# Two MoE layers on the two row halves of TensorE instead of on its column halves

## The chip, the cores and the metric

The kernel runs on one core of a Trainium2 chip. Its time is the device time of one execution in microseconds (us). A profiled execution is taken apart from the timed ones; its span runs from the first to the last instruction. TensorE is called PE in the profile (PEld is its weight loads), VectorE DVE, ScalarE ACT, GpSimd POOL and SyncE SP.

## The reference

Attention with a threshold (8 batches, 8 heads, 576 tokens, head dimension 64), followed by a two-layer perceptron over all 4608 tokens:

```python
scores = scale * np.matmul(q, k.transpose(0, 1, 3, 2))
thresh = np.max(scores, axis=-1, keepdims=True) - tau
scores = np.where(scores >= thresh, scores, -1e9)
attn = np.exp(scores - max); attn = attn / (sum + 1e-9)
x = np.matmul(attn, v)            # to (4608, 512)
h = x @ w_in                      # 512 -> 2048
out = np.maximum(0.01 * h, h) @ w_out   # 2048 -> 512
```

## The kernel before

The work is cut into 144 steps, 18 for each batch. A step takes two heads (a pair) and 128 queries: 16 steps cover the first 512 tokens, 2 "tail" steps the last 64 tokens of all eight heads. The loop at the end of the kernel (L487 to L534) runs over the steps n and issues, in this order, the work of several stages. Each engine's instructions stand in that order.

In step n, PE makes the scores of step n (`scores`, L217): q and k stand as high and low fp16 halves, so there are three products for each of two key halves and two heads, twelve matmuls. The heads of a pair lie in rows 0 to 63 and 64 to 127 of the array and run as a pair of matmuls, each on half of the rows and all 128 columns (64x128). DVE copies the scores out and takes the minimum of their negatives (`copy_min`, L225); POOL (DVE in the first 28 steps) makes the threshold (L232). ACT does two exponentials and a ramp for the step before (`exps`, L250 to L254), DVE the weights of one head (L263). Every second step the weights of two steps are turned by a DMA transpose (`turn_w`, L280) that SP issues, and four steps after the second of them, at the end of that step, PE multiplies them with v (`pv`, L303; PV_LAG = 4). DVE writes the result, with the normalizing factor, to the input x of the layers (`evacuate`, L325 and L315).

The layers work on groups of 256 tokens (128 for the tails of two batches). `layer1` (L346) makes one of eight units of h, 16 matmuls of 256 columns, followed by ACT's leaky ramp (L348); `layer2` (L362), twice a step, makes one eighth of the output of 128 tokens, four matmuls of 512 columns; ACT copies the output (L368) and SP stores it. Layer 2 of a group comes up once all units of layer 1 are issued. In both layers and in PV the output's 128 rows are split in two (`u2`), so that two matmuls run on the two column halves of the array (128 rows x 64 columns):

```python
nc.tensor.matmul(out=hp[ds(64 * u2, 64), jj, :], lhsT=w_in16[:, i, ds(128 * j + 64 * u2, 64)],
                 rhs=g.x[:, i, :], start=(i == 0), stop=(i == 3), skip_group_check=True)
```

q and k of the next batch are loaded by SP, split by POOL into high and low halves (`split_scale`, `split_high`, `split_low`), and turned by PE (`turn`, L177): 16 transposes per pair and operand (8 for the tails) into a PSUM tile `tp`, also on column halves, which DVE copies out (L188, L180). `turns_at`, `pool_at` and `loads_at` are dictionaries, written by hand, that say in which step each of these is issued.

PSUM tiles: `sc` two buffers, `h` two (hp, tp), `o` one, `pv` one.

Of the kernel before, what the change touches and what calls it, by code (L numbers as in the profile page):

```python
# [11 lines left out]
AX = mybir.AluOpType  # L12
AF = mybir.ActivationFunctionType

PV_LAG = 4


class Group:
# [20 lines left out]
def kernel(  # L39
# [122 lines left out]
    def turn(key, copy=None):  # L162
# [24 lines left out]
        else:  # L187
            copy(out=dst[:, :, p, ds(c0, 512)], in_=tp[:, :, :, :].rearrange("d x t p -> d x (t p)"))  # L188

    steps = []
# [9 lines left out]
    def scores(st):  # L202
        st.sc = [ps.tile([128, 2, 512], FP32, tag="sc", bufs=2, name=f"sc{h}") for h in range(2)]
        for kh in range(2):
            for i, (qx, kx) in enumerate(((0, 0), (1, 0), (0, 1))):
                for u in range(2 if st.tail else 1):
                    for h in range(2):
                        pair = st.p + u
                        rows = ds(64 * h, 64)
                        key0 = 64 * (1 - h) + 288 * kh  # L210
                        if st.tail:
                            lhs = turned[st.b, "q"][rows, qx, pair, MAIN:S]
                            o = st.sc[h][ds(64 * u, 64), kh, 0:288]
                        else:
                            lhs = turned[st.b, "q"][rows, qx, pair, ds(256 * st.blk + 128 * st.c, 128)]
                            o = st.sc[h][:, kh, 0:288]
                        nc.tensor.matmul(out=o, lhsT=lhs, rhs=turned[st.b, "k"][rows, kx, pair, ds(key0, 288)],  # L217
                                         start=(i == 0), stop=(i == 2), skip_group_check=True)

    def copy_min(st):  # L220

# [11 lines left out]

    def exps(st):

        c = 0 if st.tail else st.c
        if c == 0:
            pairs["now"] = pr = Pair()
            pr.w = sb.tile([128, 2, 10, 128], FP16, tag="w", bufs=3, name="w")
            pr.sum = sb.tile([128, 2, 2], FP32, tag="sum", bufs=3, name="sum")  # L240
            pr.n = 1 if st.tail else 2
        st.pair = pr = pairs["now"]
        flat = pr.w[:, c, :, :].rearrange("q n d -> q (n d)")
        st.w = [flat[:, ds(576 * h, 576)] for h in range(2)]
        st.sum = [pr.sum[:, c, h : h + 1] for h in range(2)]
        st.e = sb.tile([128, 576], FP16, tag="e", bufs=2, name="e")
        for h in range(2):
            if h:
                z = st.s[:, h, :]
                nc.scalar.activation(out=z, in_=z, func=AF.Prelu, bias=st.th[:, h, 0:1], scale=-1.0, alpha=1e20)  # L250
                nc.scalar.activation(out=st.w[h], in_=z, func=AF.Exp, bias=minus_tau[:, :], scale=1.0,  # L251
                                     accum_out=st.sum[h])
            else:
                nc.scalar.activation(out=st.e[:, :], in_=st.s[:, h, :], func=AF.Exp, bias=st.mn[:, h, 0:1],  # L254
                                     scale=-1.0)
# [38 lines left out]
    def pv(st):  # L294
        st.pv = ps.tile([128, 4, 128], FP32, tag="pv", bufs=1, name="pv")
        wt = st.pair.wt
        for u in range(2 if st.tail else 1):
            for i in range(5):
                for h in range(2):
                    blk = i if h == 0 else 9 - i  # L300
                    rhs = wt[:, 0, blk - (blk > 4), ds(64 * u, 64)] if st.tail else wt[:, :, blk - (blk > 4), :]
                    o = st.pv[ds(64 * h, 64), 0, ds(64 * u, 64)] if st.tail else st.pv[ds(64 * h, 64), 0:2, :]
                    nc.tensor.matmul(out=o, lhsT=v16[st.b % 2][:, st.p + u, blk, :], rhs=rhs,  # L303
                                     start=(i == 0), stop=(i == 4), skip_group_check=True)

    groups = {}
# [1 line left out]
    def evacuate(st, n):  # L308
        wt = st.pair.wt
        if st.tail:  # L310
            if (st.b % 2, st.c) == (0, 0):
                groups["t"] = xg = Group(128, (st.b, None))
                xg.x = sb.tile([128, NP, 128], FP16, tag="xt", bufs=2, name="xt")
            xg = groups["t"]
            nc.vector.tensor_tensor(  # L315
                out=xg.x[:, ds(st.p, 2), ds(64 * (st.b % 2), 64)],
                in0=st.pv[:, 0, :].rearrange("d (u q) -> d u q", u=2),
                in1=wt[:, 0, 9, :].rearrange("d (u q) -> d u q", u=2), op=AX.mult)
            done = (st.b % 2, st.c) == (1, 1)
# [13 lines left out]

    l1q, l2q, stores = [], [], []

    def layer1():
        g, u, nu, _ = l1q.pop(0)
        T, nj = g.tokens, 16 // nu
        if u == 0:
            g.g = sb.tile([128, 16, T], FP16, tag=f"g{T}", bufs=2 if T == 256 else 1, name="g")  # L340
        hp = ps.tile([128, nj, T], FP32, tag="h", bufs=2, name="hp")
        for jj in range(nj):
            j = nj * u + jj
            for i in range(4):
                for u2 in range(2):
                    nc.tensor.matmul(out=hp[ds(64 * u2, 64), jj, :], lhsT=w_in16[:, i, ds(128 * j + 64 * u2, 64)],  # L346
                                     rhs=g.x[:, i, :], start=(i == 0), stop=(i == 3), skip_group_check=True)
        nc.scalar.activation(out=g.g[:, ds(nj * u, nj), :], in_=hp[:, :, :], func=AF.Prelu,  # L348
                             bias=0.0, scale=1.0, alpha=0.01)
        if u == nu - 1:  # L350
            l2q.extend((g, m, r) for m in range(T // 128) for r in range(8))

    def layer2(n):
        g, m, r = l2q.pop(0)
        if r == 0 and n > N:

            g.o = ps.tile([128, 2, 512], FP32, tag="sc", bufs=2, name="osc")[:, 0, :]
        elif r == 0:
            g.o = ps.tile([128, 512], FP32, tag="o", bufs=1, name="o")
        for j in (2 * r, 2 * r + 1):  # L360
            for u2 in range(2):
                nc.tensor.matmul(out=g.o[ds(64 * u2, 64), :], lhsT=g.g[:, j, ds(128 * m + 64 * u2, 64)],  # L362
                                 rhs=w_out16[:, j, :], start=(j == 0), stop=(j == 15), skip_group_check=True)
        if r == 7:
            nm = g.tokens // 128
            if m == 0:
                g.osb = sb.tile([128, nm, 512], FP32, tag=f"osb{nm}", bufs=2 if nm == 2 else 1, name="osb")
            nc.scalar.activation(out=g.osb[:, m, :], in_=g.o[:, :], func=AF.Copy, bias=0.0, scale=1.0)  # L368
            if m == nm - 1:
                stores.append(g)  # L370

    def store():
        g = stores.pop(0)
# [12 lines left out]
    def at(d, n, f):  # L386
        d.setdefault(n, []).append(f)

    def units(b):
        u = [(b, p, w_) for p in range(NP) for w_ in "kq"]  # L390
        return u[:2] + [(b, "t", "k")] + u[2:] + [(b, "t", "q")]

    for b in range(1, B):
        base = PERB * (b - 1)
        for i, (s, w_) in enumerate(((0, "k"), (0, "q"), (1, "k"), (1, "q"))):
            at(loads_at, base + ((-2, 0, 5, 7)[i] if b > 1 else (3, 4, 8, 9)[i]),
               lambda b=b, s=s, w_=w_: load_main(b, s, w_))
        for i, w_ in enumerate("kq"):
            at(loads_at, base + (2, 12)[i] + 4 * (b == 1), lambda b=b, w_=w_: load_tails(b, w_))
        for i, key in enumerate(units(b)):  # L400
            n_ = base + 4 + 18 * i // 10 if b > 1 else 9 + 3 * i // 2
# [3 lines left out]
            at(turns_at, n_, lambda key=key: turn(key, nc.vector.tensor_copy))  # L405
    for b in range(B):
        base = PERB * (b - 1)
        if b:
# [73 lines left out]
        at(turns_at, n_, lambda key=key: turn(key, nc.vector.tensor_copy if key[2] == "q" else None))  # L482

    N = len(steps)
    pv_at = {s.n + PV_LAG - s.early: s for s in steps if s.tail or s.c == 1}
    n = 0
    while n < N + PV_LAG + 2 or l1q or l2q or stores:  # L487
        for f in loads_at.get(n, []):
# [21 lines left out]
        if 1 <= n <= N:  # L510
            last = steps[n - 1]
            weights(last)
            if last.early:
                recip(last.pair, last.c, 1)
                widen(last.pair, last.c, 1, nc.vector)
            elif last.tail or last.c == 1:
# [5 lines left out]
        if l1q and l1q[0][3] <= n:  # L522
            layer1()
        for f in turns_at.get(n, []):
            f()
        if 2 <= n < N + 2 and steps[n - 2].early:
            turn_w_pe(steps[n - 2].pair, steps[n - 2].c)
        for _ in range(2):
            if l2q:
                layer2(n)  # L530
        if n in pv_at:
            pv(pv_at[n])
            evacuate(pv_at[n], n)
        n += 1  # L534
# [1 line left out]
_INS = ['q', 'k', 'v', 'tau', 'moe_w_in', 'moe_w_out']  # L536
# [31 lines left out]
```

## Time and profile before

| | us |
|---|---|
| median of 3 runs | 515.27 (514.92 to 516.35) |
| the profiled execution | 515.1 |
| its span | 513.2 |
| PE busy | 488.5 |
| ACT busy | 433.4 |
| DVE busy | 423.8 |
| POOL busy | 305.3 |

The mean granted clock of PE was 0.992 of full speed. A busy PE is not PE at its peak: recorded matmuls overlap, and their ends are modelled. What a stage costs is read from the distance between starts.

### The profile page before, as it was taken

The numbers are of one execution on the slowest core, as the hardware profiler recorded it, in microseconds if no ns is written. First come the engines' busy times: TensorE is split into PE (matmuls) and PEld (weight loads), VectorE is DVE, ScalarE is ACT, GpSimd is POOL, SyncE is SP. The second block draws the span as 40 slices with busy tenths as digits, with TensorE's granted clock in tenths as the row PEclk, the third lists the DMA queues.
The fourth block names the chain that finished last, engine by engine and source line by source line (L and its number), as shares of the span: only waits on it lengthen the run. The fifth ranks groups of instructions, "written<-read, shape, count | busy, mean of one in ns | idle before, by whom it ended". The sixth has DMA issues, their size and how long they took to land.

```text
span 513.2 us, 19695 instructions
## 1 busy us (share of the span) xinstructions
PE 488.5 (95%) x8043; PEld 352.0 (69%) x8043; DVE 423.8 (83%) x1174; ACT 433.4 (84%) x781; POOL 305.3 (59%) x523
## 2 busy tenths in 40 slices
PE   7878798999999999999999999999999999999996
PEld 6656576657677777777676777777776777666884
DVE  4999999999898888888898888988898888888300
ACT  4977887789899989998899989998999989999532
POOL 4991578356776767666676767666776764223000
PEclk9989989999999999999999999999999999999999
DMA  8995787599989888878978999979988979666611
GB/s 246 237 204 98 146 183 151 129 190 168 239 166 183 201 188 192 173 149 210 206 178 177 203 187 192 168 156 212 183 203 159 202 166 158 135 117 138 144 43 63
DMA packets 220700, 87.79 MB, mean 171 GB/s; under 512 B 190913, under 2 KB 217537, under 8 KB 220609
## 3 DMA queue, kind: packets, MB, share of 16 engines
q1 hardware_dynamic: 217648, 82.07, 77.5%
q0 software_dynamic: 2688, 4.19, 4.7%
q8 instruction: 63, 1.03, 0.8%
q14 instruction: 29, 0.23, 0.1%
q10 hardware_dynamic: 272, 0.26, 0.1%
HBM read 36.70 MB, written 9.44 MB: 90 GB/s over the span
## 4 chain that ended last, share of the span: by engine, by line
PE 74%; DMA 4%; DVE 0%; ACT 0%; POOL 0%; issue 0%; DVEq 0%
PE hp L346 23%; PE o L362 18%; PE sc L217 18%; PE pv L303 6%; DMA wT<-w 4%; PE tp L177 4%; PE osc L362 3%; ACT osb L368 0%; DVE s L225 0%; DVE x L325 0%; POOL w L272 0%; DVE rec L269 0%; POOL half L148 0%; DVEq L325 0%; ACT s L250 0%
## 5 line engine op out<-in xcount | busy, mean ns | idle before, releaser
L225 DVE TENSOR_SCALAR_CACHE_REDUCE s<-sc 128x576 f32<-128x576 f32 x288 | 206.3, 753 | 33.6 <-PE sc L217 24.4
L346 PEld LDWEIGHTS <-win 128*64 128x64 f16 x2560 | 118.8, 110 | 35.0 <-issue 33.0
L217 PE MATMUL sc<-kT,qT 64*128 64x288 f16 (+1 forms) x1920 | 136.0, 286 | 5.3 <-DVE s L225 4.6
L346 PE MATMUL hp<-x,win 128*64 128x256 f16 x2048 | 137.6, 277 | 2.0 <-DVE x L325 2.0
L232 POOL TENSOR_SCALAR th<-mn 128x2 f32<-128x2 f32 x116 | 71.4, 616 | 113.1 <-ACT g L348 56.2
L362 PE MATMUL o<-wout,g 128*64 128x512 f16 x992 | 127.8, 379 | 0.0
L263 DVE SCALAR_TENSOR_TENSOR w<-s,th,e 128x576 f16<-128x576 f32 x144 | 126.3, 877 | 0.0
L251 ACT ACTIVATE w<-s,minus_tau 128x576 f16<-128x576 f32 x144 | 111.7, 776 | 9.4 <-DMA wT<-w 2.6
L217 PEld LDWEIGHTS <-qT 64*128 64x128 f16 (+1 forms) x1920 | 77.2, 97 | 57.2 <-issue 42.4
L250 ACT ACTIVATE s<-s,th 128x576 f32<-128x576 f32 x144 | 110.4, 767 | 4.1 <-POOL th L232 2.5
L254 ACT ACTIVATE e<-s,mn 128x576 f16<-128x576 f32 x144 | 110.2, 765 | 1.2 <-DVE s L225 1.2
L348 ACT ACTIVATE g<-hp 128x512 f16<-128x512 f32 x144 | 84.3, 586 | 28.6 <-PE hp L346 27.4
L362 PEld LDWEIGHTS <-g 128*64 128x64 f16 x1152 | 62.7, 110 | 29.7 <-issue 0.2
L148 POOL TENSOR_TENSOR half<-scaled,half 128x512 f16<-128x512 f32 (+1 forms) x75 | 79.9, 1065 | 1.7
L303 PE MATMUL pv<-wT,v 128*64 128x256 f16 (+1 forms) x960 | 54.1, 248 | 2.2 <-DMA wT<-w 2.2
L303 PEld LDWEIGHTS <-v 128*64 128x64 f16 x960 | 43.4, 111 | 18.0 <-issue 3.6
L177 PE MATMUL tp<-ident,half 128*64 128x128 f16 x1152 | 47.5, 223 | 4.3 <-DVE half L159 1.8
L272 POOL CAST w<-rec 128x256 f16<-128x256 f32 (+1 forms) x76 | 28.7, 378 | 38.3 <-DVE rec L269 35.1
L144 POOL CAST half<-scaled 128x512 f16<-128x512 f32 (+1 forms) x75 | 45.3, 604 | 7.6 <-PE tp L177 3.0
L177 PEld LDWEIGHTS <-half 128*64 128x64 f16 x1152 | 41.0, 112 | 6.7 <-issue 2.9
L138 POOL TENSOR_SCALAR scaled<-raw 128x512 f32<-128x512 f32 x60 | 38.0, 633 | 7.9 <-DMA raw<-in_k_dram 5.8
L325 DVE TENSOR_TENSOR x<-pv,wT 128x256 f16<-128x256 f32 x64 | 26.8, 419 | 7.0 <-PE pv L303 6.3
(44 smaller groups left out, 306.5 us busy)
## 6 DMA issues: line engine op xcount, KB each, us to landing
vraw<-in_v_dram SPq DMA_DIRECT2D x16, 512.0 KB, 4.7
out_dram<-osb SPq DMA_DIRECT2D x16, 512.0 KB, 4.5
raw<-in_k_dram SPq DMA_DIRECT2D x14, 512.0 KB, 4.4
raw<-in_q_dram SPq DMA_DIRECT2D x14, 512.0 KB, 4.7
win<-in_moe_w_in_dram POOLq DMA_DIRECT2D x4, 512.0 KB, 8.2
wout<-in_moe_w_out_dram POOLq DMA_DIRECT2D x4, 512.0 KB, 12.2
wT<-w SPq DMA_TRANSPOSE x76, 5.6
raw<-in_k_dram SPq DMA_DIRECT2D x4, 256.0 KB, 4.4
```

Source lines behind the costliest of these rows:

```text
L148: nc.gpsimd.tensor_tensor(out=halves[key][:, 1, 0:n, :, :], in0=scaled.pop(key)[:, 0:n, :, :], in1=halves[key][:, 0, 0:n, :, :], op=AX.sub ...
L177: nc.tensor.transpose(o, half[:, x, t, h, :], ident[:, :])
L217: nc.tensor.matmul(out=o, lhsT=lhs, rhs=turned[st.b, "k"][rows, kx, pair, ds(key0, 288)], start=(i == 0), stop=(i == 2), skip_group_check= ...
L225: nc.vector.tensor_scalar(out=st.s[:, h, :].rearrange("p (a b) -> p a b", a=2), in0=st.sc[h][:, :, 0:288], scalar1=-1.0 / UNIT, scalar2=No ...
L250: nc.scalar.activation(out=z, in_=z, func=AF.Prelu, bias=st.th[:, h, 0:1], scale=-1.0, alpha=1e20)
L251: nc.scalar.activation(out=st.w[h], in_=z, func=AF.Exp, bias=minus_tau[:, :], scale=1.0, accum_out=st.sum[h])
L254: nc.scalar.activation(out=st.e[:, :], in_=st.s[:, h, :], func=AF.Exp, bias=st.mn[:, h, 0:1], scale=-1.0)
L263: nc.vector.scalar_tensor_tensor(out=st.w[0], in0=st.s[:, 0, :], scalar=st.th[:, 0, 0:1], in1=st.e[:, :], op0=AX.is_le, op1=AX.mult, accum ...
L303: nc.tensor.matmul(out=o, lhsT=v16[st.b % 2][:, st.p + u, blk, :], rhs=rhs, start=(i == 0), stop=(i == 4), skip_group_check=True)
L346: nc.tensor.matmul(out=hp[ds(64 * u2, 64), jj, :], lhsT=w_in16[:, i, ds(128 * j + 64 * u2, 64)], rhs=g.x[:, i, :], start=(i == 0), stop=(i ...
L348: nc.scalar.activation(out=g.g[:, ds(nj * u, nj), :], in_=hp[:, :, :], func=AF.Prelu, bias=0.0, scale=1.0, alpha=0.01)
L362: nc.tensor.matmul(out=g.o[ds(64 * u2, 64), :], lhsT=g.g[:, j, ds(128 * m + 64 * u2, 64)], rhs=w_out16[:, j, :], start=(j == 0), stop=(j = ...
```

## The change

Four things change.

1. In steps where there is work for it (`by_rows`), the layers no longer split their output over column halves but their sum over row halves: layer 2 runs on one half of the rows with all 128 columns, layer 1 on the other, and the halves change places from step to step, so that each result is complete after two steps. The matmuls of the two lists are issued in an order that a small count of columns (`clock`) gives. PV of such a step is issued ahead of the layers, not behind them.
2. In these steps q and k are turned by rows (`turn_rows`): transposes of 64 tokens at a time, eight on one row half ahead of layer 2 and eight on the other between the two parts of layer 1, into a tile `tpr` that has the buffer of `pv`.
3. `wait_for`, called ahead of the first layer matmul of each such step, and `begin`, ahead of the second eight transposes, drain TensorE; `signal` does nothing.
4. PV comes five steps late, and both tail steps of a batch form a pair with one PV, one transposing DMA and one evacuation. Layer 2 may begin before all of layer 1 is issued (`ready2`), in parts of four eighths over two steps. The turns' steps (`rows_at`) and the loads of q's tails move.

In the built program 116 of the 144 steps go through `by_rows`, and 49 turns through `turn_rows`; the numbers of matmuls and weight loads on PE are the same as before (8043 each).

```diff
-PV_LAG = 4
+PV_LAG = 5
...
+    def turn_rows(keys):
+        tp = ps.tile([128, 1024], FP16, tag="pv", bufs=1, name="tpr")
...
+            for r in range(2):
+                rows = ds(64 * r, 64)
+                for x in range(2):
+                    for t in range(n):
+                        o = t_[:, x, r, t, :] if p == "t" else t_[:, x, t, rows]
+                        jobs[r].append((64, lambda o=o, half=half, x=x, t=t, rows=rows: nc.tensor.transpose(
+                            o, half[rows, x, t, :, :].rearrange("p h d -> p (h d)"), ident[rows, rows])))
...
+    def jobs1(g, u, nu, hp, half, first):
+        rows, nj = ds(64 * half, 64), 16 // nu
+        return [(g.tokens, lambda jj=jj, i=i: nc.tensor.matmul(
+            out=hp[:, jj, :], lhsT=w_in16[rows, i, ds(128 * (nj * u + jj), 128)], rhs=g.x[rows, i, :],
+            start=(first and jj + i == 0), stop=(not first and i == 3), skip_group_check=True))
+            for jj in range(nj) for i in range(4)]
...
+    def jobs2(g, m, r, half, first):
+        rows, o = ds(64 * half, 64), g.o
+        return [(512, lambda j=j: nc.tensor.matmul(
+            out=o[:, :], lhsT=g.g[rows, j, ds(128 * m, 128)], rhs=w_out16[rows, j, :],
+            start=(first and j == 0), stop=(not first and j == 15), skip_group_check=True))
+            for j in range(2 * r, 2 * r + 8)]
...
+    def signal(a):
+        return 0
+    def wait_for(a, count):
+        nc.tensor.drain()
+    def by_rows(n, keys):
+        lower = n % 2
+        one, two, after = [], [], []
+        turned_first = done = 0
+        if half2:
+            part = half2.pop()
+            two.extend(jobs2(*part, lower, False))
...
+        elif n + 1 < N and n % 2 == 0 and ready2(4):
+            half2.append(l2q[0])
...
+            two.extend(jobs2(*half2[0], lower, True))
+        if half1:
+            unit = half1.pop()
+            one.append(jobs1(*unit, 1 - lower, False))
+            after.insert(0, lambda: end1(*unit))
+        if n + 1 < N and two and l1q and l1q[0][3] <= n:
+            g, u, nu, _ = l1q.pop(0)
+            half1.append((g, u, nu, begin1(g, u, nu)))
+            one.append(jobs1(*half1[0], 1 - lower, True))
+        if keys and one and two:
+            a, b, copy = turn_rows(keys)
+            a, b = (a, b) if lower == 0 else (b, a)
...
+            def begin(f=b[0][1]):
+                nc.tensor.drain()
+                return f()
+            b[:1] = [(64, begin)]
+            two[0:0] = a
+            one.insert(1, b)
+            after.insert(0, copy)
...
+        lists, clock = [two, sum(one, [])], [0, 0]
+        while lists[0] or lists[1]:
+            t = 0 if not lists[1] or lists[0] and clock[0] <= clock[1] else 1
+            cols, f = lists[t].pop(0)
+            clock[t] = max(clock[t], clock[1 - t] - 512) + cols
+            if "scores" in mark:
+                wait_for(0, mark.pop("scores"))
+            i = f()
...
-    pv_at = {s.n + PV_LAG - s.early: s for s in steps if s.tail or s.c == 1}
+    pv_at = {s.n + PV_LAG - 2 * s.early: s for s in steps if s.c == 1}
...
+        if n < N and (half1 or half2 or one and n % 2 == 0 and ready2(4)):
+            if n in pv_at:
+                pv(pv_at[n])
+            after = by_rows(n, keys)
+            if n in pv_at:
+                evacuate(pv_at[n], n)
+            for f in after:
+                f()
```

More of the change, by code (lines that the diff above doesn't have):

```diff
@@ L188, in turn, with copy @@
             copy(out=dst[:, :, p, ds(c0, 512)], in_=tp[:, :, :, :].rearrange("d x t p -> d x (t p)"))
+    def turn_rows(keys):
+        tp = ps.tile([128, 1024], FP16, tag="pv", bufs=1, name="tpr")
+        jobs, copies = ([], []), []
+        for i, (b, p, which) in enumerate(keys):
+            dst, half = turned_of(b, which), halves.pop((b, p, which))
+            n = 2 if p == "t" else 4
+            if p == "t":
+                t_ = tp[:, ds(512 * i, 512)].rearrange("d (x u s p) -> d x u s p", x=2, u=2, s=2)
+            else:
+                t_ = tp[:, :].rearrange("d (x t p) -> d x t p", x=2, t=4)
+            for r in range(2):
[5 more added lines that the diff above has]
+                            o, half[rows, x, t, :, :].rearrange("p h d -> p (h d)"), ident[rows, rows])))
+            copies.append((dst, t_, p, which))
+        def copy():
+            for dst, t_, p, which in copies:
+                if p == "t":
+                    c0 = MAIN if which == "q" else 0
+                    for x in range(2):
+                        nc.vector.tensor_copy(out=dst[:, x, :, ds(c0, 64)],
+                                              in_=t_[:, x, :, :, :].rearrange("d u s p -> d (u s) p"))
+                    if which == "k":
+                        nc.gpsimd.tensor_copy(out=dst[:, :, :, 576:640], in_=dst[:, :, :, 0:64])
+                else:
+                    c0 = 0 if which == "q" else 64
+                    nc.vector.tensor_copy(out=dst[:, :, p, ds(c0, 512)], in_=t_.rearrange("d x t p -> d x (t p)"))
+        return jobs[0], jobs[1], copy
     steps = []
@@ L216, in scores @@
                             o = st.sc[h][:, kh, 0:288]
-                        nc.tensor.matmul(out=o, lhsT=lhs, rhs=turned[st.b, "k"][rows, kx, pair, ds(key0, 288)],
-                                         start=(i == 0), stop=(i == 2), skip_group_check=True)
+                        mm = nc.tensor.matmul(out=o, lhsT=lhs, rhs=turned[st.b, "k"][rows, kx, pair, ds(key0, 288)],
+                                              start=(i == 0), stop=(i == 2), skip_group_check=True)
+                        if (kh, i, u, h) == (0, 0, 0, 1):
+                            mark["scores"] = signal(mm)
     def copy_min(st):
@@ L234, in exps @@
     def exps(st):
-        c = 0 if st.tail else st.c
+        c = st.c
         if c == 0:
@@ L240, in exps @@
             pr.sum = sb.tile([128, 2, 2], FP32, tag="sum", bufs=3, name="sum")
-            pr.n = 1 if st.tail else 2
+            pr.n = 2
         st.pair = pr = pairs["now"]
@@ L296, in pv @@
         wt = st.pair.wt
-        for u in range(2 if st.tail else 1):
+        for c, u in [(c, u) for c in range(2) for u in range(2)] if st.tail else [(0, 0)]:
             for i in range(5):
@@ L300, in pv @@
                     blk = i if h == 0 else 9 - i
-                    rhs = wt[:, 0, blk - (blk > 4), ds(64 * u, 64)] if st.tail else wt[:, :, blk - (blk > 4), :]
-                    o = st.pv[ds(64 * h, 64), 0, ds(64 * u, 64)] if st.tail else st.pv[ds(64 * h, 64), 0:2, :]
-                    nc.tensor.matmul(out=o, lhsT=v16[st.b % 2][:, st.p + u, blk, :], rhs=rhs,
+                    if st.tail:
+                        rhs = wt[:, c, blk - (blk > 4), ds(64 * u, 64)]
+                        o = st.pv[ds(64 * h, 64), c, ds(64 * u, 64)]
+                    else:
+                        rhs = wt[:, 0:2, blk - (blk > 4), :]
+                        o = st.pv[ds(64 * h, 64), 0:2, :]
+                    nc.tensor.matmul(out=o, lhsT=v16[st.b % 2][:, 2 * c + u if st.tail else st.p, blk, :], rhs=rhs,
                                      start=(i == 0), stop=(i == 4), skip_group_check=True)
@@ L310, in evacuate @@
         if st.tail:
-            if (st.b % 2, st.c) == (0, 0):
+            if st.b % 2 == 0:
                 groups["t"] = xg = Group(128, (st.b, None))
@@ L315, in evacuate @@
             nc.vector.tensor_tensor(
[L316 to L319, printed above, removed]
+                out=xg.x[:, :, ds(64 * (st.b % 2), 64)].rearrange("d (c u) q -> d c u q", c=2),
+                in0=st.pv[:, 0:2, :].rearrange("d c (u q) -> d c u q", u=2),
+                in1=wt[:, :, 9, :].rearrange("d c (u q) -> d c u q", u=2), op=AX.mult)
+            done = st.b % 2 == 1
         else:
@@ L334, with begin1, end1 @@
     l1q, l2q, stores = [], [], []
+    def begin1(g, u, nu):
+        if u == 0:
+            g.g = sb.tile([128, 16, g.tokens], FP16, tag=f"g{g.tokens}", bufs=2 if g.tokens == 256 else 1, name="g")
+            g.nu, g.ready = nu, 0
+            l2q.extend((g, m, r) for m in range(g.tokens // 128) for r in range(8))
+        return ps.tile([128, 16 // nu, g.tokens], FP32, tag="h", bufs=2, name="hp")
+    def end1(g, u, nu, hp):
+        nj = 16 // nu
+        nc.scalar.activation(out=g.g[:, ds(nj * u, nj), :], in_=hp[:, :, :], func=AF.Prelu,
+                             bias=0.0, scale=1.0, alpha=0.01)
+        g.ready = nj * (u + 1)
     def layer1():
         g, u, nu, _ = l1q.pop(0)
[L338 to L341, printed above, removed]
+        hp = begin1(g, u, nu)
+        nj = 16 // nu
         for jj in range(nj):
@@ L347, in layer1, with begin2 @@
                                      rhs=g.x[:, i, :], start=(i == 0), stop=(i == 3), skip_group_check=True)
[L348 to L354, printed above, removed]
+        end1(g, u, nu, hp)
+    def jobs1(g, u, nu, hp, half, first):
[4 more added lines that the diff above has]
+            for jj in range(nj) for i in range(4)]
+    def begin2(g, m, r, n):
         if r == 0 and n > N:
@@ L359, in layer2, with end2, ready2 @@
             g.o = ps.tile([128, 512], FP32, tag="o", bufs=1, name="o")
+    def end2(g, m):
+        nm = g.tokens // 128
+        if m == 0:
+            g.osb = sb.tile([128, nm, 512], FP32, tag=f"osb{nm}", bufs=2 if nm == 2 else 1, name="osb")
+        nc.scalar.activation(out=g.osb[:, m, :], in_=g.o[:, :], func=AF.Copy, bias=0.0, scale=1.0)
+        if m == nm - 1:
+            stores.append(g)
+    def ready2(parts):
+        return len(l2q) >= parts and l2q[0][0].ready >= 2 * (l2q[0][2] + parts) and l2q[0][2] % parts == 0
+    def layer2(n):
+        g, m, r = l2q.pop(0)
+        begin2(g, m, r, n)
         for j in (2 * r, 2 * r + 1):
@@ L364, in layer2 @@
         if r == 7:
[L365 to L370, printed above, removed]
+            end2(g, m)
+    def jobs2(g, m, r, half, first):
[4 more added lines that the diff above has]
+            for j in range(2 * r, 2 * r + 8)]
@@ new lines @@
+    half1, half2, mark = [], [], {}
+    own = tc.alloc_semaphore("own")
+    def signal(a):
[9 more added lines that the diff above has]
+            two.extend(jobs2(*part, lower, False))
+            if part[2] == 4:
+                after.append(lambda: end2(*part[:2]))
+        elif n + 1 < N and n % 2 == 0 and ready2(4):
+            half2.append(l2q[0])
+            del l2q[:4]
+            begin2(*half2[0], n)
+            two.extend(jobs2(*half2[0], lower, True))
[10 more added lines that the diff above has]
+            a, b = (a, b) if lower == 0 else (b, a)
+            turned_first = len(a)
+            def begin(f=b[0][1]):
[5 more added lines that the diff above has]
+            after.insert(0, copy)
+        elif keys:
+            for key in keys:
+                after.insert(0, lambda key=key: turn((key), nc.vector.tensor_copy))
+        lists, clock = [two, sum(one, [])], [0, 0]
[6 more added lines that the diff above has]
+            i = f()
+            if t == 0:
+                done += 1
+                if turned_first and done == turned_first + 1:
+                    mark["half"] = signal(i)
+        return after
@@ L391, in units @@
         return u[:2] + [(b, "t", "k")] + u[2:] + [(b, "t", "q")]
+    rows_at = {}
+    ROWS = [(0, "k"), (0, "q"), ("t", "k"), ("t", "q")] + [(p, w_) for p in (1, 2, 3) for w_ in "kq"]
     for b in range(1, B):
@@ L398 @@
         for i, w_ in enumerate("kq"):
-            at(loads_at, base + (2, 12)[i] + 4 * (b == 1), lambda b=b, w_=w_: load_tails(b, w_))
-        for i, key in enumerate(units(b)):
-            n_ = base + 4 + 18 * i // 10 if b > 1 else 9 + 3 * i // 2
+            at(loads_at, base + (2, 4)[i] if b > 1 else (6, 16)[i], lambda b=b, w_=w_: load_tails(b, w_))
+        for i, key in enumerate(units(b) if b == 1 else ROWS):
+            n_ = (9, 10, 12, 13, 15, 16, 18, 19, 20, 21)[i] if b == 1 else base + (5, 7, 9, 9, 11, 13, 15, 17, 19, 21)[i]
+            key = (b,) + key[-2:]
             at(pool_at, n_ - 3, lambda key=key: split_scale(key))
@@ L404 @@
             at(pool_at, n_ - 2, lambda key=key: split_low(key))
-            at(turns_at, n_, lambda key=key: turn(key, nc.vector.tensor_copy))
+            if b == 1:
+                at(turns_at, n_, lambda key=key: turn(key, nc.vector.tensor_copy))
+            else:
+                at(rows_at, n_, key)
     for b in range(B):
@@ L515 @@
                 widen(last.pair, last.c, 1, nc.vector)
-            elif last.tail or last.c == 1:
+            elif last.c == 1:
                 recip(last.pair, 0, last.pair.n)
@@ L521 @@
             store()
[L522 to L529, printed above, removed]
+        keys = rows_at.get(n, [])
+        one = bool(l1q) and l1q[0][3] <= n
+        if n < N and (half1 or half2 or one and n % 2 == 0 and ready2(4)):
[6 more added lines that the diff above has]
+                f()
+        else:
+            two = ready2(2) and (n >= N or n % 2 == 0 or l2q[0][2] % 4 == 2)
+            if one:
+                layer1()
+            for f in turns_at.get(n, []):
+                f()
+            for key in keys:
+                turn(key, nc.vector.tensor_copy)
+            if 2 <= n < N + 2 and steps[n - 2].early:
+                turn_w_pe(steps[n - 2].pair, steps[n - 2].c)
+            for _ in range(2 * two):
                 layer2(n)
-        if n in pv_at:
-            pv(pv_at[n])
-            evacuate(pv_at[n], n)
+            if n in pv_at:
+                pv(pv_at[n])
+                evacuate(pv_at[n], n)
         n += 1
```

## Prediction

> **What bounds the kernel now.** I read the page first, then the windows of each batch of 18 steps, then the timeline of one step.
>
> ```profile
> PE 488.5 (95%) x8043; PEld 352.0 (69%) x8043; DVE 423.8 (83%) x1174; ACT 433.4 (84%) x781; POOL 305.3 (59%) x523
> ...
> PE 74%; DMA 4%; DVE 0%; ACT 0%; POOL 0%; issue 0%; DVEq 0%
> ```
>
> TensorE is busy for 95% and is the chain that ends last. The windows (busy time per engine) say where that holds:
>
> ```profile
> 74.27:134.25 59.98, 55.82 (x908) 39.36 (x906) 55.90 (x157) 50.23 (x91) 37.92 (x63) 1.00 0.87 175
> 249.34:307.05 57.71, 57.71 (x1003) 41.11 (x1002) 50.82 (x140) 51.81 (x94) 39.87 (x69) 1.00 0.92 188
> 422.39:473.40 51.01, 51.01 (x760) 35.26 (x758) 42.95 (x123) 48.26 (x90) 16.46 (x34) 1.00 0.75 142
> 473.40:508.80 35.40, 35.14 (x566) 27.46 (x564) 5.33 (x17) 16.10 (x30) 2.17 (x5) 1.00 0.31 84
> ```
>
> From step 36 (134 us) on, PE is busy in all of every window; in the first two batches it isn't, and there the other engines set the pace. After the last scores only layer work is left, again all PE. ACT needs 51.81 us of 57.71, 2.9 us a step: the next bound. One step, with the next one's start:
>
> ```profile
> 207.07 0.91 PE L217 MATMUL sc<-kT,qT 64*128 64x288 f16 x12
> 207.91 1.06 PE L346 MATMUL hp<-x,win 128*64 128x256 f16 x16
> 208.81 0.61 PE L177 MATMUL tp<-ident,half 128*64 128x128 f16 x16
> 209.26 1.03 PE L362 MATMUL o<-wout,g 128*64 128x512 f16 x8
> 210.12 0.71 PE L303 MATMUL pv<-wT,v 128*64 128x256 f16 x10
> 210.76 0.91 PE L217 MATMUL sc<-kT,qT 64*128 64x288 f16 x12
> ```
>
> Everything runs in pairs: scores on two row halves (64*128), all else on two column halves (128*64). In the records behind these lines pairs follow each other every 122.5 ns (288 columns), 109 ns (256), 216 ns (512) and 56 ns (128): the columns streamed set the rate, weight loads are hidden. The one loss is where the halving changes. Six score pairs are 0.735 us, but 0.84 passes: the last pair waits 93 ns longer than its 122.5 before the layer starts, and the layer's first pair takes 24 ns more, 0.117 us in all. From PV back to scores it is 96 + 11 ns, 0.107 us. So 0.224 us of each step is switching.
>
> **The layers side by side.** In 116 of 144 steps the two u2 halves of the columns become two halves of the rows: eight matmuls of 512 columns (layer 2) on one, sixteen of 256 (layer 1) on the other. Streamed time: 8 x 0.216 = 1.73 us, against 8 x 0.109 + 4 x 0.216 = 1.74 before. Nothing is gained or lost in streaming, if the halves overlap as the score pairs do; the loads per half are no denser than the scores' (one per 109 ns against 122.5). What is gained is that scores and layers no longer differ in halving. PV still runs on columns, every second step, now between scores and layers. A batch of 18 steps had 18 x 0.224 = 4.03 us of switching; 9 changes from scores to PV remain, 9 x 0.117 = 1.05 us. The 9 changes back to rows coincide with a drain, next.
>
> **The drains.** wait_for is a drain of TensorE, and the built program has 165: one ahead of the first layer matmul in each of the 116 steps, and 49 more in the middle of the steps that also turn q or k. In a steady batch, 18 and 9. No drain stands inside the kernel before; the only one that waits for work is its last:
>
> ```profile
> L563 PEldq DRAIN  x2: 13/1288/2563, 506.2 to 512.8; - x2
> ```
>
> It begins at 506.217 and lasts 2.563 us, to 508.780, 46 ns after the last matmul's end (508.355 + 0.379 = 508.734). After the one wait that PE's queue held amid work (at 58.70) the next load followed 25 ns after it. So I price a drain as: the last matmul's full duration (283 ns for scores, 273 for PV, 379 for 512 columns, by the records) + 46 + 25 ns, less the distance at which the next would have started (122.5, 109, 216), plus 24 ns for the first pair: 0.255, 0.259 and 0.258 us, thus 0.26 us. Nothing covers it: PE is the bound, and both halves stand still. Below, the bound is a mere flush as in a change of halving, 0.117 us; below that only a drain that waits for nothing (13 ns, the second in that row). Above, I allow 0.33 us for a queue that must fill again, an estimate: 0.26 and the 46 + 25 ns once more. I take 0.26, since the row is of the same instruction on the same engine.
> 27 x 0.26 = 7.02 us a batch.
>
> **The turns.** A unit had 16 transposes of 128 columns in pairs, 8 x 0.056 = 0.447 us; per batch 8 of these and two of half size, 72 x 0.056 = 4.03 us. Now a turn is 8 transposes of 64 columns on one row half, a drain, then 8 on the other. The built order puts the first eight ahead of four layer-2 matmuls while the other half does only eight layer-1 matmuls (0.87 us) and then waits; the second eight run alone. Both sets of eight are thus added to the path. Their rate no row shows. Nearest are the tail PVs:
>
> ```profile
> 200.50 0.48 PE L303 MATMUL pv<-wT,v 128*64 128x64 f16 x20
> 200.91 0.91 PE L217 MATMUL sc<-kT,qT 64*128 64x288 f16 x12
> ```
>
> 0.41 less the change of 0.107 leaves 0.30 us for 10 pairs: 30 ns for 64 columns with 64 columns of weights. A turn by rows has 128 columns of weights; the idle matmuls of line 462 (128 columns of each) follow every 56 ns, so a load takes no more. Between 30 and 56 I take 35, nearer the row with equal streaming. 9 x 16 x 0.035 = 5.04 us a batch (4.32 to 8.06).
>
> **The rest.** PV of both tail steps as one keeps its 40 matmuls and drops a transposing DMA (of the 76), a reciprocal and an evacuation a batch: off the path. PV five steps late starts after the scores of the fifth step rather than at the end of the fourth, about the same moment; PE waited for these DMAs 2.2 us in all. Moved loads of q's tails meet an SP queue that PE doesn't wait for. Layer 2 now may begin when half of layer 1 is done, but in pairs of steps only: by the built order, 360 layer-1 and 200 layer-2 matmuls come after the last scores' start, against 304 and 176. 56 x 54.5 ns + 24 x 108 ns = 5.6 us of work leaves steps where PE had spare time or then has too little (2.4 us against ACT's 2.9), and lands at the end, where nothing hides it.
>
> **The sum**, against the profiled execution (515.1 us, span 513.2; the median is 515.27). Steady batch: -4.03 + 1.05 + 7.02 - 4.03 + 5.04 = +5.05 us; steps 54 to 126 are four: +20.2. Steps 126 to 144 have no turns: -4.03 + 1.05 + 18 x 0.26 = +1.7. Steps 36 to 54: the drains, less the 4.3 us of work moved out, but four short steps then wait for ACT: +3. The first 36 steps: 0, since PE has 14 and 4 us to spare. The end: +5.6. Together +30.5: 546 us.
>
> **Rivals.**
> A drain costs only a flush. For: a change of halving also empties the array and costs 0.117 us. Against: the last drain ended 46 ns after the modelled end, not before. 27 x 0.143 = 3.9 us a batch less, 2.6 in the last, some 2 in steps 36 to 54: 545.6 - 20.2 = 525 us. Chance 0.13.
> The Trainium skill, "TensorEngine Tiling (Array Packing)", Key Properties, says that changing the tiling mode itself drains TensorE. The 0.117 us agree with that; by that rule the drain at PV's end would be free, and the sum about 0.14 us lower for each.
>
> The faster side: the drains wait for nothing (the 13 ns row), and the turns then overlap the layers as the issuing clock of by_rows plans, 0.22 us each. Steady batch: -4.03 + 2.1 - 4.03 + 2.0 = -4.0, near ACT's limit; four of these, -1.9 in the last, +2 in 36 to 54, +5.6 at the end: -10, 505 us. It decides only below some 0.08 us a drain. Chance 0.05.
>
> The bank of PV. tpr shares the single buffer of pv. In odd steps DVE copies it out after its two reductions and the weights, which ended 3.73 us after the scores' start in this step; PV asks for the bank about 0.85 us after the next scores start, some 4.3 us after it. With 0.5 us of slack it is free; should DVE slip by 0.8, 49 turns wait 0.3 us: +15, 561 us. Chance 0.08.
>
> The halves don't overlap: a load for a half waits for that half's matmul. Sixteen short matmuls would take 16 x (0.109 + 0.094, a score load's duration) = 3.25 us instead of 1.73: +176 over 116 steps, 690 us. Against: within the scores, loads for a row half start 11 ns after that half's matmul. Chance 0.04.
> The Trainium skill, "TensorE: Matmul & The Clock Gate", The mechanism (Part 3), says that loads overlap running matmuls only where the row group differs; by that rule the 690 us would hold, and the trace of the scores disagrees.
>
> **How the numbers follow.** The forecast has 0.70. Its own ends: with 0.26 us a drain, 30 ns give 543 and 56 ns some 559. The range 524 to 566 adds the flush below and the bank above; what is left out is 690, 505 and drains of 0.33 with turns at 56 ns (569). A difference within 0.3%, 1.5 us, is about what a measurement can't tell from no change. Faster 0.05; same 0.02, from the edge of the flush case; slower 0.93.
>
> **What would show it.** Right: steady batches near 62.8 us instead of 57.7, PE gaps of 0.25 us after scores, PV and in the middle of turns, the turns' transposes 30 to 40 ns apart, last scores to last matmul about 41 us instead of 35.4, layers still 0.216 us per long matmul. Wrong: gaps near 0.1 us (flush), a steady batch under 57 us, PE waiting for DVE ahead of PV (bank), or long matmuls over 0.3 us apart.

## The result, and the profile after

The changed kernel takes 545.54 us (545.14 to 546.19), against 515.26 before: ratio 1.0585, 95% interval 1.0566 to 1.0604. Its profiled execution has a span of 543.5 us, 30.3 more. The page's first lines again:

```profile
PE 503.1 (93%) x8043; PEld 378.3 (70%) x8043; DVE 416.5 (77%) x1158; ACT 432.9 (80%) x781; POOL 305.8 (56%) x515
...
PE 73%; issue 4%; DVE 2%; ACT 0%; POOL 0%; DVEq 0%; POOLq 0%
```

PE ends last as before, but its share fell from 95 to 93% and "issue" has 4% of the chain: time in which PE stood and waited for nothing that the profile shows. The other engines did the same work in more time. The windows of the batches (columns: PE, PEld, DVE, ACT, POOL busy, PEclk, DMA share, GB/s):

```profile
73.57:133.19 59.62, 55.58 (x857) 38.94 (x856) 54.50 (x156) 49.14 (x88) 38.45 (x62) 1.00 0.85 181
133.19:192.40 59.21, 56.56 (x939) 42.17 (x936) 49.66 (x139) 51.25 (x94) 40.01 (x68) 1.00 0.80 180
254.92:317.56 62.64, 59.86 (x1005) 45.92 (x1002) 49.95 (x139) 53.07 (x97) 40.09 (x69) 1.00 0.81 170
442.71:497.61 54.90, 52.83 (x780) 42.22 (x775) 43.25 (x123) 48.39 (x90) 18.20 (x34) 1.00 0.69 131
497.61:538.95 41.34, 41.19 (x646) 29.93 (x644) 4.66 (x13) 19.01 (x33) 1.42 (x3) 1.00 0.31 72
```

A steady batch takes 62.6 us instead of 57.8 (mean of four each), and PE, busy for all of it before, now has 2.8 us without a matmul. The end takes 41.3 instead of 35.4. Step 36 begins at 133.19 us, 1 us earlier than before. The timeline of PE in a step that turns shows where it stands; the next step's scores begin at 220.11:

```profile
216.72 0.92 PE L253 MATMUL sc<-kT,qT 64*128 64x288 f16 x12
217.75 0.20 PE L207 MATMUL tpr<-ident,half 64*128 64x64 f16 x1
...
218.43 0.38 PE L444 MATMUL o<-wout,g 64*128 64x512 f16 x1
218.54 0.27 PE L406 MATMUL hp<-x,win 64*128 64x256 f16 x1
218.64 0.38 PE L444 MATMUL o<-wout,g 64*128 64x512 f16 x1
219.10 0.32 PE L207 MATMUL tpr<-ident,half 64*128 64x64 f16 x5
219.24 0.39 PE L444 MATMUL o<-wout,g 64*128 64x512 f16 x1
```

Two holes: the scores' last pair starts at 217.36, the next matmul at 217.75 instead of 217.48; and from 218.64, the start of a matmul that streams for 0.216 us, nothing starts until 219.10. Between them long matmuls follow every 0.216 us with two short ones beside each: the halves overlap. The weight loads run along: here is a load of the short matmuls' half, at the start of that half's own matmul.

```profile
218.10 0.20 PEld L406 LDWEIGHTS <-win 64*128 64x128 f16 x2
```

The row of the 116 drains that `wait_for` issues (PEldq is the queue of PE's loads):

```profile
L458 PEldq DRAIN  x116: 543/1426/1820, 88.9 to 497.7; - x116
```

Their durations (1.4 us) are no price, since PE's queue reaches a drain long before the array does. The price is the distance of starts around each: about 396 ns after scores instead of 122.5, with a turn behind the drain or without; 384 after PV instead of 109; 457 in the middle of a turn instead of 216. A drain ends 52 ns after the last matmul's recorded end (21 ns after a long one's), and the next load starts 53 ns later.

### The profile page after: what moved, and what is told of

It reads as the page before. It is cut to its first block, busy times and chain, and to the rows that moved or that the text cites. A ratio compares the mean times of both kernels' runs of the same rounds, so it can differ in the third digit from the quotient of the medians.

```text
span 543.5 us, 19791 instructions
## 1 busy us (share of the span) xinstructions
PE 503.1 (93%) x8043; PEld 378.3 (70%) x8043; DVE 416.5 (77%) x1158; ACT 432.9 (80%) x781; POOL 305.8 (56%) x515
## 4 chain that ended last, share of the span: by engine, by line
PE 73%; issue 4%; DVE 2%; ACT 0%; POOL 0%; DVEq 0%; POOLq 0%
PE o L444 19%; PE hp L406 18%; PE sc L253 15%; PE pv L345 7%; PE tpr L207 6%; PE hp L399 3%; PE osc L436 3%; DVE s L263 1%; PE o L436 1%; DVE w L301 1%; DVE x L367 0%; ACT s L288 0%; ACT e L292 0%; POOL th L270 0%; POOL half L144 0%
## 5 line engine op out<-in xcount | busy, mean ns | idle before, releaser
L444 PE MATMUL o<-wout,g 64*128 64x512 f16 x896 | 220.2, 377 | 7.1
L406 PE MATMUL hp<-x,win 64*128 64x256 f16 x1600 | 199.4, 270 | 0.4
L406 PEld LDWEIGHTS <-win 64*128 64x128 f16 x1952 | 159.5, 94 | 13.4 <-issue 1.9
L253 PE MATMUL sc<-kT,qT 64*128 64x288 f16 (+1 forms) x1920 | 146.0, 285 | 6.2 <-DVE s L263 5.0
L253 PEld LDWEIGHTS <-qT 64*128 64x128 f16 (+1 forms) x1920 | 102.7, 97 | 25.7 <-issue 14.5
L444 PEld LDWEIGHTS <-g 64*128 64x128 f16 x896 | 74.5, 94 | 25.2 <-issue 22.9
L207 PEld LDWEIGHTS <-half 64*128 64x128 f16 x784 | 28.1, 95 | 47.8 <-issue 27.6
L207 PE MATMUL tpr<-ident,half 64*128 64x64 f16 x784 | 39.3, 191 | 10.3 <-DVE x L367 0.6
L310 POOL CAST w<-rec 128x256 f16<-128x256 f32 x68 | 27.2, 399 | 31.7 <-DVE rec L307 31.1
L422 ACT ACTIVATE osb<-o 128x512 f32<-128x512 f32 x31 | 18.5, 597 | 22.8 <-PE o L444 21.3
```

What stands on the lines that cost most here:

```text
L207: jobs[r].append((64, lambda o=o, half=half, x=x, t=t, rows=rows: nc.tensor.transpose(o, half[rows, x, t, :, :].rearrange("p h d -> p (h d ...
L253: mm = nc.tensor.matmul(out=o, lhsT=lhs, rhs=turned[st.b, "k"][rows, kx, pair, ds(key0, 288)], start=(i == 0), stop=(i == 2), skip_group_c ...
L406: return [(g.tokens, lambda jj=jj, i=i: nc.tensor.matmul(out=hp[:, jj, :], lhsT=w_in16[rows, i, ds(128 * (nj * u + jj), 128)], rhs=g.x[row ...
L444: return [(512, lambda j=j: nc.tensor.matmul(out=o[:, :], lhsT=g.g[rows, j, ds(128 * m, 128)], rhs=w_out16[rows, j, :], start=(first and j ...
```

## The experiments

My theory: the halves overlap as forecast and all that is lost is the drains (165) and the transposes that run with one half idle. The rivals: a drain is no more than the flush of a change of halving; the row halves themselves are slow; the bank that turns share with PV makes PE wait for DVE; the rest of the change costs. Dropping the drains alone wasn't tried: both row halves would write the same PSUM bank with no order between them. What the drains kept in order had to be ordered in another way. All ratios are against the kernel before.

**The rest of the change without row halves** (cols).

```diff
-        if n < N and (half1 or half2 or one and n % 2 == 0 and ready2(4)):
+        if False:
```

> The changed kernel with the condition for by_rows never true: layers and turns on column halves in every step, no drain, the rest of the change kept (PV five steps late, both tails as one, layer 2 from half of layer 1 on). Theory (the row halves with their drains are the whole loss): about 515 us, 512 to 518, steady batches 57.7 us, last scores to last matmul about 36 us (the built order leaves 320 and 168 layer matmuls for it, before 304 and 176). Rival (the late PV, the moved loads or the joined tails cost something): 520 us or more, with PE waiting for the transposing DMA or for DVE.

Measured: 516.31 us, ratio 1.0014 (1.0001 to 1.0026). Taken together, late PV, joined tails, moved loads and the earlier layer 2 are worth less than 1 us; the 29 us lie in by_rows. It is a balance, though, and not the neutral change that I expected: step 36 begins at 130.1 us, 4 us earlier than before, and a steady batch takes 58.5 us, 0.7 more than before. There two turns share a step, and PE waits for ACT to free a buffer of `h`, once in each of the four steady batches (total in us, times, longest):

```profile
PE tp L177 <- ACT g L387: 2.6, 4, 0.8
```

**A drain in the kernel before** (before_drain).

```diff
+            if n < N:
+                nc.tensor.drain()
             layer1()
```

> The kernel before with a drain of TensorE added ahead of layer 1 in the 130 steps that have one before the last scores; there the halving changes from rows to columns already. Theory (a drain waits for the last matmul's end, and the queue then starts anew, so 396 ns from score pair to layer pair as in the changed kernel, against 216 now): 0.18 us each, 106 of them where PE is the bound: +19, 534 us. Rival (a drain is a flush, as the change of halving is): nothing added, 515 us.

Measured: 539.57 us, ratio 1.0464 (1.0443 to 1.0484); a batch takes 61.4 us instead of 57.8. The timeline has the same pair of lines as before the change:

```profile
259.03 0.91 PE L217 MATMUL sc<-kT,qT 64*128 64x288 f16 x12
260.08 1.06 PE L346 MATMUL hp<-x,win 128*64 128x256 f16 x16
```

1.05 us from scores to layer, where it was 0.84. In a place where the halving changes anyway, a drain adds 0.205 us. A drain thus costs more than the change of halving, and the rival falls; my 0.18 was too low because here the drain ended 78 ns after the last matmul, not 52. The Trainium skill, "TensorEngine Tiling (Array Packing)", Key Properties, says that a change of tiling mode drains TensorE; the trace agrees that the change costs something (0.117 us). Were that the same wait as the instruction's, the added drain would have been free here, and it wasn't.

**Two drains for one** (two_drains).

```diff
         nc.tensor.drain()
+        nc.tensor.drain()
```

> The changed kernel with a second drain right behind each of the 116; it has nothing to wait for. What it adds is what the instruction itself costs in the queue. If the 53 ns from a drain's end to the next load are paid for each drain: about 100 x 0.053, +5, 551 us. If they are paid once for the restart of the array: no more than 13 ns each (the empty drain of the page), +1, 547 us. If most of the price is in the instruction and not in waiting for the last matmul: +0.25 each, 570 us.

Measured: 554.98 us, ratio 1.0757 (1.0734 to 1.0781), 9.4 us above the changed kernel.

```profile
L459 PEldq DRAIN  x116: 13/13/13, 88.5 to 506.9; - x116
```

The second drain has a duration of 13 ns in every case, and yet the distance from score pair to layer grows from 396 to 474 ns, from PV from 384 to 464. So the instruction takes 80 ns of the queue with nothing to wait for, more than the 53 that I allowed and six times its recorded duration. If a first drain costs the queue as much, which no run shows, 80 ns of its 0.27 us are the instruction, and the rest is the wait for the last matmul to leave the array.

**Order by a read instead of a drain** (reads_for_drains). At the end of a step DVE copies one column of o and of hp; the other half's matmuls into these banks have to wait for that read.

```diff
-        nc.tensor.drain()
+        pass
...
+            after.append(lambda o=g2.o: nc.vector.tensor_copy(out=seen[:, 0:1], in_=o[:, 0:1]))
...
+            after.append(lambda hp=half1[0][3]: nc.vector.tensor_copy(out=seen[:, 1:2], in_=hp[:, 0, 0:1]))
```

> The changed kernel without its 116 drains ahead of the layers; the order that they gave comes from reads by DVE of one column of o and hp at the end of the step (seen, two small copies), which the next half's matmuls have to wait for. The 49 drains amid turns stay. Theory (drains price the loss): 0.29 us less in 56 steps and 0.175 less in the 60 with PV, where the change of halving stays; some 14 of them in the first 36 steps, where PE isn't the bound: -24, about 521 us, steady batches 58.3 us. Rival (flush): -56 x 0.117 = -7, 539 us. Rival (the row halves themselves are slow, or DVE's reads come late): 540 us or more.

Measured: 523.28 us, ratio 1.0145 (1.0126 to 1.0164): 22 us less with 116 drains less. The window of a steady batch:

```profile
247.38:306.30 58.92, 58.18 (x1005) 46.40 (x1001) 52.00 (x170) 52.30 (x96) 40.12 (x69) 1.00 0.94 185
```

58.9 us (58.5 in the next), against 62.6. The reads cost DVE 2 us a batch and PE little: some 15 ns in most odd steps, and 0.3 us in steps 73 and 137, where a read came late (the batch shown has the first of them). This settles the main part: the row halves aren't slow, the drains are.

**The turn's drain shared** (turn_shared_drain).

```diff
-            b[:1] = [(64, begin)]
-            two[0:0] = a
-            one.insert(1, b)
+            for _, f in a:
+                f()
+            one.insert(0, b)
```

> The changed kernel with the first eight transposes of a turn moved ahead of the step's own drain and the second eight behind it, beside layer 2; the 49 drains amid turns go, 116 stay. Theory: a turning step is 0.735 + 0.24 + 0.29 + 1.745 + 0.24 = 3.25 us instead of 3.39: -0.14 x 42 in the part where PE is the bound, about -6, 539 us. Rival (the transposes or the shared bank of PV make the turning step long, not its drain): 545 us, no change, with waits for DVE ahead of PV.

Measured: 533.04 us, ratio 1.0333 (1.0313 to 1.0353), 12.5 us less than the changed kernel and twice what I expected. A pair of steps with a turn takes 6.64 us instead of 6.91: 0.26 us for a drain that had cost 457 - 216 = 241 ns. My own sum for the step (3.25 us) had put both sets of transposes on the path; in the trace the second set runs beside layer 2, and layer 1 on its half finishes beside the next scores. The window of a steady batch:

```profile
249.08:309.49 60.41, 58.67 (x1003) 49.43 (x1002) 49.94 (x139) 53.19 (x96) 40.12 (x69) 1.00 0.88 176
```

**Turns by columns** (turns_by_cols).

```diff
-        if keys and one and two:
+        if False:
```

> The changed kernel with all turns on column halves again, behind the layers; layers on row halves with their 116 drains as they are. Theory: a turning step is 0.735 + 0.27 (drain) + 1.73 + 0.117 + 0.447 + 0.107 = 3.41 us, as long as the 3.39 of turns by rows with a drain in their middle: 546 us, 543 to 549; turning by rows brings nothing as long as it needs its drain. Rival (turns by rows save the 16 x 64 columns that they no longer stream): 12 us slower, 557 us. Rival (the bank that turns by rows share with PV costs): 540 us or less.

Measured: 548.12 us, ratio 1.0621 (1.0604 to 1.0639), 2.6 us above the changed kernel. Nearly equal: turning by rows with a drain in the middle brings next to nothing. A turning step takes 3.46 us against 3.39, and the step behind it 3.42 against 3.52. Most of the 2.6 us are waits: four times, 2.3 us in all, PE waits for DVE where two turns share a step.

**No drain at all** (no_drains; no_drains_late begins with row halves at step 54).

```diff
+        if rows_now and rows_at.get(n) and half1 and half2:
+            a, b, copy = turn_rows(rows_at.pop(n))
...
+            for _, f in a:
+                f()
...
+            nc.vector.tensor_copy(out=seen[:, 0:2], in_=mark["tpr"][:, c0 : c0 + 2])
...
         if n < N:
             scores(steps[n])
```

> No drain at all: order by DVE's one-column reads, and a turn's first eight transposes stand ahead of the scores, ordered by a read of DVE too, the second eight beside layer 2; PV's evacuation ahead of the weights on DVE. Theory: a turn costs 0.24 + 0.24 us, in the kernel with reads for drains 0.70 (pair of steps 6.44 against 5.74 without a turn): -0.22 x 9 a batch from 58.5 to 56.5, 513 us, at last below the kernel before, whose batch is 57.7. Rival (the read of the first eight, or the evacuation ahead of them, comes late and PE waits for DVE): 520 us or more.

> As the kernel without drains, but by rows only from step 54 on; until then layers and turns go by columns as before, where PE had to wait for ACT in steps without layer 2. Theory: the 2 to 3 us lost in steps 36 to 54 come back: 511 us. Rival (those steps wait for something else): no change from the kernel without drains.

Measured: 515.53 us, ratio 0.9989 (0.9975 to 1.0003), and 515.55 us, 0.9993 (0.9981 to 1.0005). Both are the time of before, short of what I expected; a batch takes 57.8 us, not 56.5. The two largest waits of PE between 190 and 440 us name the cause, which the prediction had as a rival and which had not shown until then (total in us, times, longest):

```profile
PE pv L346 <- DVE qT L223: 2.6, 15, 0.2
PE pv L346 <- DVE kT L223: 2.1, 13, 0.2
```

PV waits for DVE's copy of the turned tile, which holds the bank of pv. With the drains gone the steps became short enough for that copy, last in DVE's step, to come late: behind most turns PV starts 1.21 us after its scores do, where 0.98 is enough without the wait (next experiment). In the profile of the changed kernel this wait does not occur.

**The copy ahead of the weights** (copy_first, and copy_first_late from step 54 on).

```diff
+            after = by_rows(n, rows_at.get(n, []))
+            if turned_now:
+                after.pop(0)()
         if 1 <= n <= N:
             last = steps[n - 1]
             weights(last)
```

> The kernel without drains, with DVE's copy of the turned tile ahead of its weights instead of behind them (and the layers of the step issued ahead of the weights, so that the copy may stand there). Theory: there PV starts 1.21 us after the scores instead of 0.98, because it waits for that copy to free the bank of pv, nine times a batch: 9 x 0.23 = 2.1 us less of 57.75, 55.7 a batch, and over the 106 steps from step 36 on about -10: 506 us, below the kernel before. Rival (the bank isn't what PV waits for, or the weights come too late for the transposing DMA): 513 to 516 us, no change.

> The same with the row halves from step 54 on only. Theory: eight units less of the gain of turns and a few steps without waits for ACT, about even: 507 us, 504 to 510. Rival (PV waits for something else): 515 us.

Measured: 511.21 us, ratio 0.9921 (0.9907 to 0.9935), and 511.26 us, 0.9920 (0.9907 to 0.9934). That is 0.8% below the kernel before, clear of the noise, and a good 4 us below the kernels without drains, where about 9 had been expected. One batch in the window:

```profile
301.31:358.00 56.69, 56.69 (x940) 47.72 (x938) 53.60 (x180) 52.08 (x95) 40.13 (x69) 1.00 0.95 189
```

The other steady batches take 56.6, 57.8 and 56.8 us; in the one of 57.8 PV waits twice for the transposing DMA, 0.9 us, as the rival had it.

Where all is in time, PV again starts 0.98 us after its scores: steps 59 and 60 together fell by the whole 0.23 us (6.34 to 6.10). Most turns aren't in time. DVE, with its reads, is now busy for 53.6 of 56.7 us, and its read of a turn's first eight transposes, which the second eight have to wait for, comes late. In step 91, whose scores start at 304.97 us:

```profile
305.34 0.13 DVE L511 COPY seen<-o 128x1 f32<-128x1 f32 x1
305.66 0.16 DVE L513 COPY seen<-hp 128x1 f32<-128x1 f32 x1 [0.20 <-issue]
305.74 0.15 DVE L651 COPY seen<-tpr 128x2 f16<-128x2 f16 x1
305.94 0.30 PE L208 MATMUL tpr<-ident,half 64*128 64x64 f16 x5
```

In 25 of the 38 turns from step 55 on, the second eight start 52 or 53 ns after that read ends, later than the 0.75 us after the scores at which they mostly start elsewhere, by up to 0.63 us; in the kernel without drains this is so in 2 of the 38. These pairs of steps take 6.17 to 6.73 us, 0.25 more on average than 6.10. So the wait for DVE has in part moved from the copy to the read. That is of the size of the missing 5 us (25 x 0.25), but no run undoes it, so it isn't shown to be all.

Row halves from the start or from step 54 make no difference: what the early start wins in steps 36 to 54 (55.4 us against 57.5) it loses in the batch behind them (56.6 against 54.7).

## Why the prediction was right

Forecast 546, measured 545.5, in the terms of its sum.

- **Streaming**: as put. Long matmuls follow every 0.216 us on one half with two short ones beside them. The rule of "TensorE: Matmul & The Clock Gate" in the Trainium skill, The mechanism (Part 3), that loads overlap only with another row group's matmuls, fails here: a load of the short matmuls' half starts at 218.10 beside that half's own matmul of 218.10, and the matmuls still follow every 0.109 us.
- **Drains**: 0.26 us put; 0.274 after scores (396 - 122.5), 0.275 after PV, 0.241 in turns. For a batch 18 x 0.275 + 9 x 0.241 = 7.1 us, put 7.02. The composition was less right than the sum: the queue's part is 53 ns and not 25, and the last matmul's end is waited for less where it is a long one.
- **Turns**: 35 ns put, 29 to 30 measured between transposes of one half: the row with equal streaming (30 ns, the tail PV) was the nearest, and the width of the weights made no difference that shows. 0.7 us a batch too much.
- **Not priced**: the scores of the tails run on quarters of the array (64*64), behind layers on row halves (64*128). Ahead of each of them the first scores start 199 ns after the last layer matmul instead of 80, so that the two steps ahead of tail scores take 0.12 us more each than others of their kind (2.89 against 2.77, 3.56 against 3.44), 0.24 us a batch.
- A steady batch so comes to -4.03 + 1.05 + 7.1 - 4.03 + 4.3 + 0.24 = +4.6; +5.05 was put, +4.8 measured.
- **Steps 126 to 144**: +1.7 put, +3.9 measured, the one term far off. I had taken them to have no turns, but the first two turning steps of the row are still in them, and a pair without turns costs 0.265 us more (3.436 + 2.771 against 3.245 + 2.698), where the drains' price gave 0.19. One PV more falls into them, too: I had put the start of the late PV at about the same moment, but it lies in the next step, so that one moves in from the batch ahead and none moves out (step 142 has a PV and takes 3.56 us, where before it has none and takes 2.72).
- **The end**: +5.6 put, +5.9 measured (41.34 against 35.40). **Steps 36 to 54**: +3 put, +2.2 measured. **The start up to step 36**: 0 put, -1.1 measured.

So the mechanism was the one forecast, and the sum held to 0.5 us partly by luck, because small errors of both signs met. Of the rivals, the flush and the drains that wait for nothing fell by the measured 0.24 to 0.28 us each and by the added drains, and the halves overlap (that rival's 690 us had left out the 30 us of the sum itself; with them it is some 721). The bank of PV cost nothing in this kernel; that rival came true once the drains were gone, at 0.23 us a turn where it had put 0.3.

## What to carry to other kernels

When two ways of halving the array alternate, price the change of halving (0.22 us for both here) before rearranging the work, and price just as carefully what keeps the new order safe: the drains, of 0.24 to 0.28 us, cost 7.1 us a batch where 3 us of changes were saved. An engine that has time can order another's writes by reading one column of the bank; here that took 22 us off and cost PE almost nothing, as long as the engine was early with its reads; where it was nearly full, PE waited for them. After such a step look at the waits again, since a buffer that was free while the steps were long becomes the next thing waited for.

## What I had not expected of the hardware

A drain with nothing to wait for is recorded with 13 ns and adds 80 ns to the distance of the matmuls around it. A drain in a place where the halving changes still adds 0.205 us to the change's 0.117. Transposes of 64 columns with weights of 128 columns on 64 rows follow each other every 29 to 30 ns.
